# Five input buffers of their own, blank rows in four transfers, and expert 0's weights loaded during attention

## The chip, the cores and the metric

One core of one Trainium2 chip runs the whole program in one launch. The metric is device time in microseconds (us); lower is better. Three runs of the kernel before gave 385.97, 389.21 and 391.08 us; their median is 389.21 us.

## What is computed

The reference is a gated linear attention (a recurrence over time, 4 batches, 8 heads, 768 steps, head size 48) followed by a hierarchical mixture of experts over the 3072 resulting tokens of width 384. Each token goes to one of 4 groups and in it to one of 4 experts, so to one of 16 experts of inner width 1024. All data are float32.

```
for t in range(S):
    state = alpha[:, :, t, :, None] * state + einsum('bhd,bhe->bhde', k[:, :, t], v[:, :, t])
    y[:, :, t] = einsum('bhd,bhde->bhe', q[:, :, t], state)
x = y as (B*S, H*D)
...
g_idx = argmax(x @ w_group);  e_idx = argmax(x[mask_g] @ w_expert[g])
h = maximum(x @ w1[g, e], 0);  out = (softmax weight of group * of expert) * (h @ w2[g, e])
```

## The kernel before, in words

The work has two stages. The first, attention, walks over 24 chunks of 128 time steps (6 chunks for each of 4 batches; called c0 to c23 here). The second runs the experts one after the other on the rows that attention has sorted by expert into a DRAM table `slots_d`.

**A chunk.** One chunk's input is a single row block of 128 x 1925 float32 (962.5 KB): decays, keys, queries and values side by side. `load` (L452) brings it into an SBUF tile that `home` (L442) picks. VectorE then runs a backward scan of the decays (`back`, L460), a reciprocal (`turn`, L466) and a forward scan (`forth`, L471). GpSimd multiplies keys (`keys`, L476) and queries (`queries`, L480) in place, in the input tile itself. TensorE takes the scores (`scores`, L494), turned keys (L523), the rows and gate logits of an earlier chunk (`to_rows`, L583), the state's gain (L536), and the output of the chunk before: `outputs` (L560) and `from_before` (L569). VectorE or ScalarE and GpSimd mask the scores (L503; L508 and L511), and VectorE adds the gain to the state (`grown`, L545). An input tile is in use until its chunk's L569 (or L560, where a batch starts) is done.

**Sorting.** Every few chunks a group's gate is computed on VectorE (L649 to L688), TensorE counts tokens per expert (L761 to L769), and GpSimd scatters each chunk's rows to `slots_d` with an indirect DMA (L737). Before the first scatter the rows from 144 to 223 of each expert's block are filled with blanks by `fill` (L803, issued at L805).

**Buffers.** Input tiles come from two places. Chunks 0 to 5 and 10 to 23 use a pool `inp` of NIN = 6 buffers; chunks 6 to 9 borrow the four weight buffers of the pool `wp` (`HOMES`, L439), which the experts need only later. So the load of chunk n waits for chunk n-10 up to n = 15 and for chunk n-6 from n = 16 on.

**Order.** Each engine runs its instructions in program order. A planner (`Plan`, L30) lays that order out from estimated costs: `add` gives every operation an engine, a cost, what it comes after, and when a transfer lands; `order` then picks, engine by engine, the ready operation with the longest path behind it. TensorE (row "pe") and the DMA queue of SyncE (row "sp") are chained in the order in which the code adds them. On SP that order is the list `order` at L858 to L866: all loads, with `wr`, the two blank fills (before loads 9 and 11) and at the end expert 0's `w1` and `w2` (`load_w1` L255, `load_w2` L261). The DMA for chunk n is told to the planner at L870.

**Into the experts.** While the last chunks run, 96 rows of expert 0 are fetched early and run on TensorE between the last chunks (L275 into the `zs` banks). Then the fullest other expert is chosen ("ahead"), its weights are loaded and, once every scatter has landed, its rows are fetched (L789); from there TensorE runs the expert products (L275 into `bank`) without a break to the end.

The few lines that set which buffer a chunk gets, and what its load waits for:

```
HOMES = {6: "w1", 7: "w2", 8: "w1", 9: "w2"}
LATER = max(HOMES) + 1
...
o = n - (LATER if n < LATER + NIN else NIN)
dma(f"load{n}", 0.45, partial(load, chunks[n]), IW * 512,
    after=[late(o, "own_out"), late(o, "gain"), late(o, "from"), late(o, "turn_k"),
           late(o, "score")], lands=0.6 if n < LATER + NIN else 2.0)
```

## Time and profile before

| | us |
|---|---|
| median of three runs | 389.21 |
| lowest, highest | 385.97, 391.08 |
| the profiled execution's own time | 387.43 |
| its span, first to last instruction | 385.7 |
| granted TensorE clock, mean over the span | 0.994 |
| TensorE busy in the span | 370.1 (96%) |
| VectorE, ScalarE, GpSimd busy | 158.2, 118.0, 201.6 |

The profile is of one execution. Times in it run from the first instruction. "PE" is TensorE, "DVE" VectorE, "ACT" ScalarE, "POOL" GpSimd, "SP" SyncE, whose work here is to issue DMAs. A wait in square brackets is the idle time of the engine just ahead of the row, with what ended it; "issue" means that the profile shows nothing that the engine waited for.

### The profile page before, as it was taken

Reading aid. Unit: us, or ns where it says so; the run is one execution under the profiler, and the core shown is the slowest. Engines: PE = TensorE matmul, PEld = TensorE weight load, DVE = VectorE, ACT = ScalarE, POOL = GpSimd, SP = SyncE. Lnnn points to the kernel's source line nnn. Section 1 sums busy time; section 2 is a strip of 40 time slices with the busy share of each in tenths; the row PEclk is TensorE's granted clock in tenths of the full one; section 3 lists DMA queues with packets and bytes.
Section 4 is the critical chain, followed back from the end, with each engine's and each line's share of the span. In section 5 each row is a group of like instructions: output and inputs, shape, how many; then the busy total and the mean of one; then the engine's idle time right before and its main releaser. Section 6 shows DMA issues by size and latency. Waiting matters only on the chain.

```text
span 385.7 us, 9827 instructions
## 1 busy us (share of the span) xinstructions
PE 370.1 (96%) x3946; PEld 352.5 (91%) x3946; DVE 158.2 (41%) x340; ACT 118.0 (31%) x310; POOL 201.6 (52%) x239
## 2 busy tenths in 40 slices
PE   8899899999899899999999999999999999999993
PEld 5787788887689899999999999999999999999993
DVE  6799589899977402020741202022021020120120
ACT  2566476766563121111112112121111121121120
POOL 5988769989697021534426153362541632623543
PEclk9999899999999999999999999999999999999999
DMA  8999905879968697856758686586876866865400
GB/s 292 392 401 399 389 29 193 289 269 294 370 237 317 182 339 262 263 204 215 222 195 257 228 274 208 192 250 248 279 212 205 301 243 211 278 263 202 181 18 32
DMA packets 30495, 94.82 MB, mean 246 GB/s; under 512 B 17925, under 2 KB 19843, under 8 KB 26096
## 3 DMA queue, kind: packets, MB, share of 16 engines
q1 hardware_dynamic: 24560, 83.53, 62.2%
q0 software_dynamic: 4832, 9.55, 7.3%
q10 hardware_dynamic: 1056, 1.10, 0.9%
q8 instruction: 32, 0.52, 0.6%
q14 instruction: 15, 0.12, 0.1%
HBM read 82.61 MB, written 11.98 MB: 245 GB/s over the span
## 4 chain that ended last, share of the span: by engine, by line
PE 84%; POOL 5%; issue 4%; DVE 3%; DMA 1%; ACT 1%; SPq 0%; POOLq 0%; DVEq 0%
PE bank L275 63%; PE bank L583 4%; PE zs L494 4%; PE zo L560 4%; PE zs L275 2%; PE zo L569 2%; POOL in L480 2%; PE zo L523 2%; PE bank L536 1%; DMA in<-in_rows_dram 1%; DVE kd L460 1%; POOL slots_d L737 1%; POOL out_dram L1174 1%; POOL in L476 1%; DVE cq L471 1%
## 5 line engine op out<-in xcount | busy, mean ns | idle before, releaser
L1174 POOL DMA_INDIRECT out_dram<-yq,dst_q x101 | 98.1, 971 | 156.0 <-DVE yq L1170 107.3
L275 PE MATMUL bank<-hT,w 128*128 128x216 f32 (+14 forms) x720 | 120.8, 328 | 0.0
L275 PEld LDWEIGHTS bank<-hT,w 128*128 128x128 f32 x720 | 118.7, 190 | 0.0
L275 PE MATMUL bank<-xt_e,w 128*128 128x213 f32 (+14 forms) x720 | 117.4, 323 | 0.0
L275 PEld LDWEIGHTS bank<-xt_e,w 128*128 128x128 f32 x720 | 115.4, 190 | 0.0
L1200 DVE SCALAR_TENSOR_TENSOR dst_q<-xq,past_q 128x7 int32<-128x7 int32 (+1 forms) x14 | 2.3, 167 | 156.5 <-DMA out_dram<-yq,dst_q 156.5
L290 ACT ACTIVATE hT<-bank 128x432 f32<-128x432 f32 (+15 forms) x64 | 31.2, 488 | 96.1 <-PE bank L275 96.1
L306 ACT COPY yT<-bank 128x432 f32<-128x432 f32 (+29 forms) x30 | 12.1, 402 | 104.4 <-PE bank L275 104.4
L737 POOL DMA_INDIRECT slots_d<-xr,place x24 | 24.1, 1005 | 8.2 <-issue 4.8
L476 POOL TENSOR_TENSOR in<-in,kd 112x512 f32<-112x512 f32 (+1 forms) x21 | 23.8, 1136 | 5.1 <-DMA in<-in_rows_dram 2.7
L583 PE MATMUL bank<-wr,yt 112*64 112x116 f32 x384 | 25.4, 275 | 0.7 <-issue 0.4
L460 DVE TENSOR_TENSOR_SCAN kd<-in,starts 112x516 f32<-112x516 f32 (+1 forms) x21 | 24.3, 1162 | 4.0 <-DMA in<-in_rows_dram 4.0
L1167 DVE STREAM_TRANSPOSE yq<-yT 128x672 f32<-128x672 f32 (+2 forms) x16 | 12.9, 809 | 31.8 <-ACT yT L306 31.8
L494 PE MATMUL zs<-in 48*64 48x128 f32 x640 | 22.2, 272 | 3.8 <-POOL in L480 3.8
L480 POOL TENSOR_TENSOR in<-in,cq 112x512 f32<-112x512 f32 (+1 forms) x22 | 23.9, 1091 | 3.4 <-DVE cq L471 3.3
L471 DVE TENSOR_TENSOR_SCAN cq<-in,starts 112x516 f32<-112x516 f32 (+1 forms) x22 | 24.7, 1129 | 1.6
L583 PEld LDWEIGHTS bank<-wr,yt 112*64 112x64 f32 x384 | 19.7, 140 | 4.4 <-issue 0.9
L494 PEld LDWEIGHTS zs<-in 48*64 48x64 f32 x640 | 18.2, 133 | 6.0 <-POOL in L480 5.5
L560 PE MATMUL zo<-sm,in 128*48 128x128 f32 (+1 forms) x320 | 22.6, 274 | 0.4 <-ACT kt L528 0.2
L575 ACT COPY yt<-zo 112x512 f32<-112x512 f32 x24 | 14.1, 586 | 21.5 <-PE zo L569 19.9
L560 PEld LDWEIGHTS zo<-sm,in 128*48 128x48 f32 (+1 forms) x320 | 18.5, 130 | 0.5 <-issue 0.3
L511 POOL TENSOR_SCALAR_AFFINE_SELECT sm<-sm 128x512 f32<-128x512 f32 x27 | 16.9, 639 | 3.0 <-ACT sm L508 2.9
(158 smaller groups left out, 345.5 us busy)
## 6 DMA issues: line engine op xcount, KB each, us to landing
w<-in_w_dram SPq DMA_DIRECT2D x34, 1536.0 KB, 6.9
in<-in_rows_dram SPq DMA_DIRECT2D x17, 962.5 KB, 11.9
w<-in_rows_dram SPq DMA_DIRECT2D x4, 962.5 KB
xq<-slots_d SPq DMA_DIRECT2D x28, 85.8 KB, 6.2
xq<-slots_d SPq DMA_DIRECT2D x28, 73.5 KB, 6.4
slots_d<-blank SPq DMA_DIRECT2D x2, 980.0 KB
out_dram<-yq,dst_q POOLq DMA_INDIRECT x101, 4.8
in<-in_rows_dram SPq DMA_DIRECT2D x1, 704.0 KB
```

The costliest lines, as they stand in the source:

```text
L275: nc.tensor.matmul(z, lhsT=w, rhs=x, start=first, stop=last, skip_group_check=True)
L290: nc.scalar.activation(out=hT[:, f0:f0 + 2, 0:n], in_=z[:, 0:2 * n].rearrange("p (f t) -> p f t", f=2), func=AF.Relu)
L460: nc.vector.tensor_tensor_scan(out=flat(c.kd[:, p0:p1])[:, ::-1], data0=c.t[0:R, A1 * p1:A1 * p0:-1], data1=one_col.to_broadcast([R, A1 * ...
L471: nc.vector.tensor_tensor_scan(out=flat(c.cq[:, p0:p1]), data0=c.t[0:R, A1 * p0:A1 * p1], data1=starts[0:R, A1 * p0:A1 * p1], initial=1.0, ...
L476: nc.gpsimd.tensor_tensor(out=c.k[:, p0:p1], in0=c.k[:, p0:p1], in1=c.kd[:, p0:p1, 1:A1], op=ALU.mult)
L480: nc.gpsimd.tensor_tensor(out=c.q[:, p0:p1], in0=c.q[:, p0:p1], in1=c.cq[:, p0:p1, 1:A1], op=ALU.mult)
L494: nc.tensor.matmul(c.zs[i][s, p, :], lhsT=c.k[r, p, s], rhs=c.q[r, p, :], start=True, stop=True)
L511: nc.gpsimd.affine_select(out=c.sm[:, i], in_=c.sm[:, i], pattern=[[0, HP], [1, P]], compare_op=ALU.is_ge, fill=0.0, base=0, channel_multi ...
L560: nc.tensor.matmul(of(c.zo, p)[o], lhsT=c.v[:, h * D:h * D + o.stop - o.start], rhs=c.sm[:, i, p, :], start=(p < 2), stop=(c.bc == 0), ski ...
L583: nc.tensor.matmul(z[s, p * W:(p + 1) * W], lhsT=c.yt[:, p, s], rhs=wr[:, p, :], start=True, stop=True)
L737: sent = nc.gpsimd.indirect_dma_start(out=slots_by[t], out_offset=bass.IndirectOffsetOnAxis(ap=m["place"][:, c:c + 1], axis=0), in_=xr[:, ...
L1174: nc.gpsimd.indirect_dma_start(out=out_by.popleft().rearrange("n (j w) -> (n j) w", j=4), out_offset=bass.IndirectOffsetOnAxis(ap=dst[:, b ...
```

## The change

Three things change. The four borrowed buffers go (`HOMES` and `LATER`) and the pool `inp` shrinks from 6 buffers to 5, so that the load of every chunk n from 5 on waits for chunk n-5. The blank rows go out in four transfers of half the size, ahead of loads 7, 8, 9 and 10. Expert 0's `w1` and `w2`, which no longer have to wait for the borrowed buffers, are issued ahead of loads 14 and 17. The planner is told that each load lands 2.0 us after its transfer.

```
-    NIN = 6
+    NIN = 5
...
-        HOMES = {6: "w1", 7: "w2", 8: "w1", 9: "w2"}
-        LATER = max(HOMES) + 1
-
         def home(c):
             if not hasattr(c, "t"):
-                if c.n in HOMES:
-                    t = wp.tile([P, DC, F], F32, name=HOMES[c.n]).rearrange("p c f -> p (c f)")
-                else:
-                    t = inp.tile([P, IW], F32, name="in")
-                c.t, c.v = t, t[:, AW + 2 * KW:IW]
+                c.t = t = inp.tile([P, IW], F32, name="in")
+                c.v = t[:, AW + 2 * KW:IW]
...
-        FILLS = 2
+        FILLS = 4
...
-        for i, k in enumerate((9, 11)):
+        for i, k in enumerate((7, 8, 9, 10)):
             before_load(k, ("fill", i))
-        order += [("w1", 0), ("w2", 0)]
+        before_load(14, ("w1", 0))
+        before_load(17, ("w2", 0))
         for kind, n in order:
             if kind == "load":
-                o = n - (LATER if n < LATER + NIN else NIN)
+                o = n - NIN
                 dma(f"load{n}", 0.45, partial(load, chunks[n]), IW * 512,
                     after=[late(o, "own_out"), late(o, "gain"), late(o, "from"), late(o, "turn_k"),
-                           late(o, "score")], lands=0.6 if n < LATER + NIN else 2.0)
+                           late(o, "score")], lands=2.0)
```

On TensorE not one instruction changes its place; only the names of the buffers that chunks 6 to 9 are read from differ. On SP the order does change. The two pieces below are SP's queue from the load of c4 to that of c10, before and after. L454 and L448 are the same line of `load`, L805 and L799 that of `fill`; a wait on PE is the wait for an earlier chunk to leave its buffer, one on DMAHW is for an earlier transfer.

Before:

```order
L454 DMA in_295<-in_rows_dram 128x1925 [waits DMAHW5_49]
L454 DMA in_342<-in_rows_dram 128x1925 [waits DMAHW6_49]
L454 DMA w1_400<-in_rows_dram 128x1925 [waits DMAHW7_49]
L454 DMA w2_438<-in_rows_dram 128x1925 [waits DMAHW0_49]
L454 DMA w1_492<-in_rows_dram 128x1925 [waits DMAHW1_49]
L805 DMA slots_d_66<-blank_86 80x8x392 [waits DMAHW2_49,Pool_49]
L454 DMA w2_591<-in_rows_dram 128x1925 [waits DMAHW3_49]
L454 DMA in_655<-in_rows_dram 128x1925 [waits DMAHW4_49,PE_49,Pool_49]
```

After:

```order
L448 DMA in_295<-in_rows_dram 128x1925 [waits DMAHW5_49]
L448 DMA in_342<-in_rows_dram 128x1925 [waits DMAHW0_49,DMAHW6_49,PE_49,Pool_49]
L448 DMA in_402<-in_rows_dram 128x1925 [waits DMAHW2_49,DMAHW7_49,PE_49,Pool_49]
L799 DMA slots_d_66<-blank_86 80x4x392
L448 DMA in_485<-in_rows_dram 128x1925 [waits DMAHW1_49,PE_49,Pool_49]
L799 DMA slots_d_66<-blank_86 80x4x392
L448 DMA in_569<-in_rows_dram 128x1925 [waits DMAHW3_49,PE_49,Pool_49]
L799 DMA slots_d_66<-blank_86 80x4x392 [waits DMAHW4_49]
L448 DMA in_655<-in_rows_dram 128x1925 [waits DMAHW5_49,PE_49,Pool_49]
L799 DMA slots_d_66<-blank_86 80x4x392 [waits DMAHW6_49]
L448 DMA in_729<-in_rows_dram 128x1925 [waits DMAHW7_49,PE_49,Pool_49]
```

Before, the first load that waits for TensorE is that of c10; after, it is that of c5, and every fill stands behind a load that waits.

Expert 0's weights, on SP after the change, from the load of c13 to that of c17 (L255 is `w1`, L261 `w2`); before, both stand behind the load of c23.

```order
L448 DMA in_972<-in_rows_dram 128x1925 [waits DMAHW2_49,DMAHW3_49,PE_49,Pool_49]
L255 DMA w1_1032<-in_w1_dram 128x3072
L448 DMA in_1106<-in_rows_dram 128x1925 [waits DMAHW4_49,DMAHW5_49,PE_49,Pool_49]
L448 DMA in_1154<-in_rows_dram 128x1925 [waits DMAHW7_49,PE_49,Pool_49]
L448 DMA in_1249<-in_rows_dram 128x1925 [waits DMAHW0_49,DMAHW6_49,PE_49,Pool_49]
L261 DMA w2_1286<-in_w2_dram 128x3072
L448 DMA in_1358<-in_rows_dram 128x1925 [waits DMAHW1_49,PE_49,Pool_49]
```

Neither weight transfer waits for anything, so each goes out right behind the load ahead of it and stands in front of the next load's data.

On DVE the planner puts the scans of a chunk later against the other work. The pieces are DVE's queue around c12's first scan (it reads `in_782` before and `in_890` after); `sm` is the masked score of c10, `sums` the state of c9.

Before:

```order
L460 SCALAR_TENSOR_TENSOR kd_1015<-in_782,starts_118 112x516
L503 TENSOR_TENSOR sm_1039<-zs0_988,causal_68 128x512
L466 RECIPROCAL starts_118<-kd_1015 112x4
L471 SCALAR_TENSOR_TENSOR cq_1016<-in_782,starts_118 112x516
L545 TENSOR_TENSOR sums_1075<-state1_120,bank_1043 112x192
```

After:

```order
L497 TENSOR_TENSOR sm_1045<-zs0_982,causal_68 128x512
L454 SCALAR_TENSOR_TENSOR kd_1058<-in_890,starts_118 112x516
L460 RECIPROCAL starts_118<-kd_1058 112x4
L465 SCALAR_TENSOR_TENSOR cq_1059<-in_890,starts_118 112x516
L539 TENSOR_TENSOR sums_1108<-state1_120,bank_1035 112x192
```

The scan of c12 now stands behind the mask of c10 instead of ahead of it; if its load is late, the state of c9 waits behind it.

On POOL the clearing of two result buffers (L418) moves from between two of the last scatters to a place ahead of c11's keys.

## Rows read from the trace of the kernel before

**Rows 1.** Chain that ended last, in order of time: start us, us, what

```profile
132.31 242.24 PE bank L275 x1488
...
380.51 0.97 POOL out_dram L1328
```

**Rows 2.** Busy time by stage; after POOL: PEclk, DMA share, GB/s

```profile
core 0: us, PE busy (x) PEld busy (x) DVE busy (x) ACT busy (x) POOL busy (x), PEclk, DMA share, GB/s
...
30.00:40.00 10.00, 9.80 (x223) 8.57 (x221) 9.54 (x13) 6.66 (x18) 8.42 (x19) 1.00 1.03 402
...
50.00:60.00 10.00, 10.00 (x240) 8.89 (x238) 8.88 (x21) 7.12 (x24) 6.78 (x7) 1.00 0.12 43
...
90.00:100.00 10.00, 8.83 (x200) 7.58 (x189) 9.69 (x16) 6.58 (x17) 9.34 (x10) 1.00 0.94 326
```

**Rows 3.** Timeline of PE, 36 to 48 us: start us, us, instruction [idle before]

```profile
36.63 1.07 PE L494 MATMUL zs<-w 48*64 48x128 f32 x32
...
40.44 0.89 PE L494 MATMUL zs<-w 48*64 48x128 f32 x24
42.69 0.45 PE L494 MATMUL zs<-w 48*64 48x128 f32 x8 [1.36 <-issue]
...
47.95 0.29 PE L494 MATMUL zs<-w 48*64 48x128 f32 x4
```

**Rows 4.** Busy time by stage in finer cuts, columns as in rows 2

```profile
40.00:42.00 2.00, 1.33 (x33) 1.00 (x30) 0.80 (x2) 1.33 (x6) 1.93 (x9) 1.00 1.02 409
...
44.00:46.00 2.00, 2.00 (x33) 2.00 (x30) 0.00 (x0) 1.75 (x4) 1.14 (x2) 0.50 0.99 412
...
93.00:97.00 4.00, 3.28 (x69) 2.73 (x67) 3.79 (x9) 2.62 (x9) 3.78 (x5) 1.00 1.02 354
```

**Rows 5.** DMA queues, from the page

```profile
q8 instruction: 32, 0.52, 0.6%
```

**Rows 6.** Timeline of DVE, 96 to 100 us

```profile
96.24 2.95 DVE L728 TENSOR_TENSOR early_held<-seen 128x1 f32<-128x1 f32 x1
...
99.28 0.14 DVE L731 TENSOR_TENSOR seen<-seen,starts 128x1 f32<-128x1 f32 x1
```

**Rows 7.** Timeline of POOL and PE, 100 to 111 us

```profile
100.64 1.18 POOL L476 TENSOR_TENSOR in<-in,kd 112x512 f32<-112x512 f32 x1 [0.89 <-DVE kd L460]
...
103.77 1.01 POOL L737 DMA_INDIRECT slots_d<-xr,place  x1 [1.95 <-DVE xr L688]
...
110.84 1.21 PE L494 MATMUL zs<-in 48*64 48x128 f32 x32 [0.27 <-POOL in L480]
```

**Rows 8.** Timeline of POOL, 113 to 116 us

```profile
114.48 1.28 POOL L418 MEMSET yT<- 128x672 f32 x2
```

**Rows 9.** Timeline of PE, 60 to 74 us: c8's buffer free, c13 to c15

```profile
51.76 0.66 PE L569 MATMUL zo<-w,state 48*48 48x128 f32 x16
...
64.88 1.06 PE L494 MATMUL zs<-in 48*64 48x128 f32 x32
...
68.68 1.11 PE L494 MATMUL zs<-in 48*64 48x128 f32 x32
...
73.01 1.07 PE L494 MATMUL zs<-in 48*64 48x128 f32 x32
```

**Rows 10.** DMA issue of one load alone (issued at 73.3 us), us to landing

```profile
in<-in_rows_dram SPq DMA_DIRECT2D x1, 962.5 KB, 7.7
```

**Rows 11.** DMA issues, from the page: KB each, median us to landing

```profile
w<-in_w_dram SPq DMA_DIRECT2D x34, 1536.0 KB, 6.9
in<-in_rows_dram SPq DMA_DIRECT2D x17, 962.5 KB, 11.9
```

**Rows 12.** Chain, c2 from its first scan to its scores

```profile
10.33 1.15 DVE kd L460
...
14.32 1.21 PE zs L494 x31
```

## The prediction

> **What bounds the kernel now.** I read the chain that ended last first. From 132.31 us on it is one unbroken piece of expert products on TensorE, 242.24 us long, and then the last scatter to DRAM at 380.51 [rows 1]. Nothing in the change touches an instruction behind 132.31, so only the time up to there can move: about 132 of the 385.7 us of the span. Around the span lie 387.43 - 385.7 = 1.7 us.
>
> The busy time by stage comes next [rows 2]. In 30 to 40 us the DMA share is 1.03, so the DMA engines have no room at all: ten chunks' inputs and the blank rows are queued ahead of need. From 50 to 60 us they stand nearly still (0.12): every buffer is full. TensorE is busy all of 50 to 60 us, and less than all of 90 to 100 us (8.83 of 10), where the share is 0.94. So attention is bound by TensorE, whose pitch I take as the distance of the scores of c14 and c15: 73.01 - 68.68 = 4.33 us [rows 9]. What the change can give is where TensorE falls short of that pitch.
>
> There are two such places. The first is in the timeline of TensorE [rows 3]: after 24 of the 32 products of c8's scores it stands still for 1.36 us. No semaphore stands between the 24th and the 25th, and the profile names no releaser. Then it works on at half clock: the granted clock is 0.50 in 44 to 46 us, which is 1.2 instead of 2.4 GHz, after a pause in 40 to 42 us in which it was busy 1.33 of 2 us [rows 4]. From c8's scores to c9's it is 47.95 - 40.44 = 7.51 us, 3.2 over the pitch: 1.36 us of pause and 1.8 of slow clock. The DMA share there is 1.02 [rows 4].
>
> The second is on VectorE: an addition on a 128 x 1 tile takes 2.95 us, while the next one of the same shape takes 0.14 [rows 6]. Behind it stand the scans of c22 and, on GpSimd, its keys (0.89 us of waiting) and a scatter (1.95) [rows 7]. The DMA share then is again 1.02 [rows 4], as the last inputs and expert 0's weights come in together.
>
> **The change part by part.**
>
> *Five buffers, first effect: no deep queue of transfers at 40 us.* After the change SP issues at most one load for each chunk that TensorE finishes, so in 4.33 us one load (0.986 MB, 2.5 us at 402 GB/s) and in four of the intervals a fill (0.5 MB, 1.2 us): 3.7 of 4.33 us, where now it is all of it. Instructions come over the same DMA engines: the page lists a queue for them, 32 packets and 0.52 MB [rows 5]. A pause in the middle of a group that waits for nothing, with the engines full, is what a late piece of program would look like. I take the pause and the slow clock as gone: -3.2 us, with 0 and -3.2 as bounds. No other work hides them: TensorE is busy without a gap right behind them (10.00 of 10 in 50 to 60 us) [rows 2], and so it is TensorE again that is late next.
>
> The Trainium skill speaks against this: "Runtime: NRT & Kernel Launch", section "Instruction fetch mechanics", says that each sequencer fetches the next block of its program over its own DMA queue while it runs the present one, and that the cost of a block's end is mostly hidden. By that the pause is no fetch, nothing here would take it away, and the sum below would be 3.2 us higher. The trace leaves it open: it shows one pause of this kind on TensorE, and that in the stretch with the fullest queue.
>
> *Five buffers, second effect: a load has less time.* The load of c13 waits for c8's last read, which ends at 51.76 + 0.66 = 52.42, and c13's scores start at 64.88 [rows 9]: 12.5 us. What has to fit: the transfer, which for one load issued alone took 7.7 us from issue to landing [rows 10]; and two scans, a reciprocal and the query product, for c2 14.32 - 10.33 = 4.0 us from first scan to scores [rows 12]. That is 11.7, so 0.8 us are left. Shorter landings are possible: a weight transfer of 1536 KB lands in 6.9 us [rows 11], and 573.5 KB less at 402 GB/s make that 5.4 us, an estimate; then 3.1 us are left. What can go wrong stands in the order: VectorE's scan of c12 now comes behind the mask of c10, and if the load is late, the state of c9 queues behind it, for which ScalarE and TensorE's output of c10 wait. GpSimd may also have another product of 1.18 us [rows 7] ahead of the query: then 0.4 us are missing for each of the 11 chunks from c12 to c22, +4.2 us. The median landing of 11.9 us [rows 11] comes from the deep queue of today, which goes. A gain isn't possible here, for no load starts earlier. I take 0, because the row of the same transfer still fits, and keep 0 and +4.2.
>
> The Trainium skill would leave more room: "DMA: Bandwidth & Descriptors", section "Anatomy of one DMA", gives a fixed 2.0 us and the bytes at 436 GB/s, so 4.3 us for a load (an estimate from that page). By that the wait would fit with over 4 us to spare, the next term would be 0, and the sum -4.1 instead of -2.8. The row (7.7 us) says otherwise here, and the row decides.
>
> *Expert 0's weights amid attention.* Both are gone from the end of the queue, and each 1.57 MB (3.9 us at 402 GB/s) now stands in front of an input: behind the loads of c13 and c16. 2.5 + 3.9 us of transfers stand ahead of a load that is issued 4.33 us after the first of them, so the loads of c14 and c17 come about 2.1 us late. For c14 the scatters have hardly begun (share 0.12) [rows 2], so I set its landing at 5.4 + 2.1 = 7.5, which with 4.0 fits into 12.5. For c17, with scatters alongside, 7.7 + 2.1 + 4.0 = 13.8 is 1.3 us too much. I take +1.3. The bounds are 0 and both at 1.3 with the slow clock behind each pause (1.8 us) [rows 3]: +6.3.
>
> What goes at the end of the queue is worth something if VectorE's 2.95 us are also a matter of full DMA engines: 2.8 us over the 0.14 of its like, and GpSimd waited 0.89 + 1.95 = 2.8 us for it. But the loads of c22 and c23 remain in that stretch. So the bounds are 0 and -2.8, and I take a third, -0.9.
>
> *Fills and clears.* Four fills move the same bytes as two, in 1.2 us pieces that fit behind a load, and none is needed before the first scatter, which comes behind c11's keys: 0. The two clears (1.28 us) [rows 8] leave GpSimd's last scatters, but the very last scatter waits for c23's own rows, which come after them anyway: 0, at best -1.3. ScalarE's order changes by a few places and it is the least busy engine (118.0 us): 0.
>
> **Sum.** -3.2 + 0 + 1.3 - 0.9 + 0 = -2.8 us. Against the profiled execution that is 387.43 - 2.8 = 384.6. That execution lies 1.8 us below the median of the runs, 389.21, so for the median I forecast 389.2 - 2.8 = 386.4 us. Rivals are given against the median, too.
>
> **Rivals.**
>
> *The pause stays, or comes again elsewhere.* For it: only one pause is in the first 48 us, though the engines were full for most of them, so a full queue alone doesn't make one. Weights and inputs that now come together at c13 and c16 fill the engines as well. Against it: none shows in the 242 us of expert products, where the engines are less loaded. Then 3.2 us are lost from the sum: 389.2 - 0.9 + 1.3 = 389.6 us. The Trainium skill's section on instruction fetch, named above, is on this rival's side. This is the case in which the change doesn't do what it says.
>
> *All of it works.* Landings near 5.4 us, no pause at c17, and VectorE's 2.95 us go wholly: -3.2 - 2.8 = -6.0, so 383.2 us; with the clears -7.3 and 381.9. For it: both stalls lie where the DMA share is over 1. Against it: the row of 7.7 us. The Trainium skill's section on the anatomy of a DMA is on this side.
>
> *Late loads pace attention; this one is slower.* Place: VectorE's first scan of a chunk, from c12 on. Price: 0.4 us for each of 11 chunks, 4.2, and at c14 and c17 a pause of 1.3 with 1.8 of slow clock behind it, 6.3; with the pause at c8 gone, 4.2 + 6.3 - 3.2 = +7.3, so 396.5 us. If that pause stays too, 399.7. It decides from the point where landing takes more than 12.5 - 4.0 = 8.5 us, or 7.3 with a product of GpSimd ahead. For it: the row of 7.7 lies between these two. Against it: half the loads, up to c11, come before the scatters, and VectorE's order has the scans later, so that less of its other work queues behind a late load.
>
> **How the numbers follow.** My chances: the forecast (384.5 to 388.5 us) 0.50, the pause stays 0.20, all of it works 0.15, late loads 0.15. For the range I leave out the upper part of the last and the best end of the third: 381.9 to 393.5 us. Over 2% (about what a measurement of this kernel can tell from no change) is 7.8 us. Faster by that needs 381.4 or less, which is even beyond the -7.3 of all gains together: 0.05 for what I don't see. Slower by that means over 397.0: 0.07, somewhat under half of the late loads. Within 2%: 0.88.
>
> **What would show it.** Right: TensorE's 32 products of c8's scores in one piece, clock 1.00 in every slice from 40 to 50 us, c9's scores about 3 us earlier; a DMA share well under 1 between 20 and 48 us; the expert products starting near 129.5 instead of 132.31. VectorE's waits for input DMAs from c12 on would be a few tenths, and over 1 us only at c14 or c17. Wrong: if the pause is there with a share under 0.9, it isn't the queue; if VectorE waits 1 us or more for most inputs, the third rival holds; if the clock falls once more between 50 and 110 us, the weights cost more than I took.

## The result, and the profile after

The changed kernel is slower, by 0.7%, which is inside the 2% for which I had given 0.88. In 20 runs of each its median is 390.66 us (388.94 to 394.64) against 388.24 (385.52 to 391.08) for the kernel before; the ratio is 1.0071, with a 95% interval of 1.0042 to 1.0099. Ratios in this document leave out the executions that took over 1.5% more than the fastest of their kernel. I had forecast 386.4 us, 2.8 less than the median I started from. The number lies inside the range I gave (381.9 to 393.5), but the kernel moved the other way.

The profiled execution took 390.86 us, 3.43 more than the one before (0.7% of the median are 2.8 us, so about 0.7 us of the layout below is the draw of the two executions). Its chain that ended last, in order of time (start us, us, what):

```profile
23.85 8.70 DMA in<-in_rows_dram
32.64 1.24 DVE kd L454
...
37.41 7.44 DMA in<-in_rows_dram
44.95 1.23 DVE kd L454
...
49.87 0.30 DVE starts L643
...
51.65 0.26 DVE picked L658
...
52.51 1.13 DVE kd L454
...
135.75 242.24 PE bank L275 x1488
```

The expert products take 242.24 us as in [rows 1] and start 3.44 us later (135.75 for 132.31). So all of it was lost in attention, the part in which the prediction had said that the time can move. The rows above it tell of two links that were not on the path before: transfers of inputs (c7's, 8.70 us, and c10's, 7.44; between 15 and 60 us before, no input's transfer was), and from 44.95 to 57.27 us a stretch of VectorE, with the first group's gate (L643 to `picked`) between the scan of c10 and that of c11 (52.51).

The pause that the change was to remove is nearly gone. TensorE after, 41 to 59 us: start us, us, instruction, idle before (to be laid beside [rows 3]; L488 is L494 of before).

```profile
41.34 1.09 PE L488 MATMUL zs<-in 48*64 48x128 f32 x26 [0.27 <-POOL in L474]
42.80 0.44 PE L488 MATMUL zs<-in 48*64 48x128 f32 x6 [0.38 <-issue]
...
46.47 1.07 PE L488 MATMUL zs<-in 48*64 48x128 f32 x32
...
52.05 0.20 PE L755 MATMUL bank<-picked,before 128*128 128x96 bf16 x1 [1.11 <-DVE picked L658]
...
52.66 1.11 PE L488 MATMUL zs<-in 48*64 48x128 f32 x32
...
58.49 1.21 PE L488 MATMUL zs<-in 48*64 48x128 f32 x32 [0.64 <-POOL in L474]
```

c8's scores are still cut, after 26 of 32 products, but for 0.38 us instead of 1.36, and from c8's scores to c9's it is 5.13 us (46.47 - 41.34) instead of 7.51. That is 2.38 us won. Then it goes wrong: TensorE waits 1.11 us for VectorE's `picked`, 0.64 for GpSimd, and c11's scores start at 58.49 (57.30 before).

The windows show the same:

```profile
core 0: us, PE busy (x) PEld busy (x) DVE busy (x) ACT busy (x) POOL busy (x), PEclk, DMA share, GB/s
...
20.00:30.00 10.00, 9.44 (x222) 8.18 (x213) 9.04 (x13) 6.63 (x21) 9.19 (x17) 1.00 0.89 262
30.00:40.00 10.00, 9.42 (x212) 8.18 (x213) 5.85 (x8) 6.25 (x17) 5.18 (x11) 1.00 1.00 344
40.00:50.00 10.00, 9.36 (x206) 8.07 (x201) 7.35 (x12) 6.53 (x20) 9.31 (x18) 1.00 0.76 269
50.00:60.00 10.00, 7.54 (x164) 5.89 (x158) 9.48 (x24) 4.44 (x13) 6.55 (x8) 1.00 0.82 310
```

The clock is 1.00 in all four. But the DMA engines are as full in 30 to 40 us as before (1.00) while they move 344 GB/s instead of 402 [rows 2], and in 50 to 60 us TensorE is busy 7.54 of 10 us, where it had been 10.00 [rows 2].

What came in place of the pause is on VectorE, whose first scan of c7 to c10 waits for its input, 2.32 + 1.47 + 1.36 + 0.95 = 6.1 us:

```profile
32.64 1.23 DVE L454 TENSOR_TENSOR_SCAN kd<-in,starts 112x516 f32<-112x516 f32 x1 [2.32 <-DMA in<-in_rows_dram]
...
37.06 1.23 DVE L454 TENSOR_TENSOR_SCAN kd<-in,starts 112x516 f32<-112x516 f32 x1 [1.47 <-DMA in<-in_rows_dram]
...
41.21 1.23 DVE L454 TENSOR_TENSOR_SCAN kd<-in,starts 112x516 f32<-112x516 f32 x1 [1.36 <-DMA in<-in_rows_dram]
...
44.95 1.23 DVE L454 TENSOR_TENSOR_SCAN kd<-in,starts 112x516 f32<-112x516 f32 x1 [0.95 <-DMA in<-in_rows_dram]
```

These loads are slow beside the fills. The list of DMA issues (KB each, median us from issue to landing), asked for the stretch in which c7's load goes out (23 to 26 us), and for that of c12's (46 to 48 us):

```profile
in<-in_rows_dram SPq DMA_DIRECT2D x1, 962.5 KB, 8.7
slots_d<-blank SPq DMA_DIRECT2D x1, 490.0 KB, 9.7
...
in<-in_rows_dram SPq DMA_DIRECT2D x1, 962.5 KB, 4.6
```

With a fill ahead of it and one behind, a load lands after 8.7 us; with none, after 4.6. The same load shows it too: c10's takes 7.44 us here, with a fill ahead of it, and 5.0 in e2 below, where the fills go out 4 us behind it.

Laid out by the starts of the scores (after minus before), the 3.44 us are: +0.90 up to c8, -2.38 from c8 to c9, +3.49 from c9 to c12, 0 to c16, +1.30 from c16 to c17, +1.17 to c19, -0.91 to c23, -0.13 to the expert products.

The +1.30 lie where the prediction had +1.3, behind the weights, but they are not a wait for c17's input. Its load does come late: it is issued at 70.85 us, and VectorE's scan waits 1.12 us for it. TensorE, though, has no idle time ahead of c17's scores. It stops inside those of c16:

```profile
79.30 0.63 PE L488 MATMUL zs<-in 48*64 48x128 f32 x12
80.79 0.88 PE L488 MATMUL zs<-in 48*64 48x128 f32 x20 [0.86 <-issue]
81.60 0.60 PE L517 MATMUL zo<-ident,in 112*128 112x112 f32 x4
```

From the first of these scores to the products behind them (L517) it is 2.30 us; before it was 1.00 (77.29 to 78.29). That is the whole 1.30, and the chain that ended last runs through this stop and not through c17's load.

### The profile page after: what moved, and what is told of

It is laid out like the page before. It is cut to its first block, busy times and chain, and to the rows that moved or that the text cites. A ratio compares the mean times of both kernels' runs of the same rounds, so it can differ in the third digit from the quotient of the medians.

```text
span 388.9 us, 9820 instructions
## 1 busy us (share of the span) xinstructions
PE 369.7 (95%) x3946; PEld 351.5 (90%) x3946; DVE 159.2 (41%) x340; ACT 118.0 (30%) x310; POOL 201.8 (52%) x239
## 4 chain that ended last, share of the span: by engine, by line
PE 78%; DVE 9%; DMA 6%; issue 3%; POOL 2%; ACT 1%; SPq 0%; POOLq 0%; DVEq 0%; ACTq 0%
PE bank L275 62%; DMA in<-in_rows_dram 6%; PE zs L488 3%; PE bank L577 3%; PE zo L554 3%; DVE kd L454 2%; PE zs L275 2%; PE zo L563 2%; DVE cq L465 1%; PE bank L530 1%; PE zo L517 1%; DVE sm L497 1%; POOL in L474 1%; POOL out_dram L1169 1%; DVE early_held L722 1%
## 5 line engine op out<-in xcount | busy, mean ns | idle before, releaser
L306 ACT COPY yT<-bank 128x432 f32<-128x432 f32 (+29 forms) x30 | 12.1, 403 | 104.3 <-PE bank L275 104.3
L470 POOL TENSOR_TENSOR in<-in,kd 112x512 f32<-112x512 f32 (+1 forms) x25 | 28.6, 1144 | 14.2 <-DVE kd L454 8.1
L454 DVE TENSOR_TENSOR_SCAN kd<-in,starts 112x516 f32<-112x516 f32 (+1 forms) x25 | 29.4, 1180 | 11.9 <-DMA in<-in_rows_dram 11.3
L488 PE MATMUL zs<-in 48*64 48x128 f32 x768 | 28.0, 272 | 6.5 <-POOL in L474 5.3
L488 PEld LDWEIGHTS zs<-in 48*64 48x64 f32 x768 | 22.5, 133 | 9.9 <-POOL in L474 7.4
L465 DVE TENSOR_TENSOR_SCAN cq<-in,starts 112x516 f32<-112x516 f32 (+1 forms) x26 | 29.6, 1144 | 1.9
L474 POOL TENSOR_TENSOR in<-in,cq 112x512 f32<-112x512 f32 (+1 forms) x26 | 28.7, 1108 | 2.4 <-DVE cq L465 2.2
L554 PE MATMUL zo<-sm,in 128*48 128x128 f32 (+1 forms) x384 | 26.8, 274 | 0.1
L554 PEld LDWEIGHTS zo<-sm,in 128*48 128x48 f32 (+1 forms) x384 | 22.1, 130 | 0.3 <-ACT kt L522 0.3
L569 ACT COPY yt<-zo 112x512 f32<-112x512 f32 x24 | 14.1, 586 | 18.2 <-PE zo L563 16.6
L543 ACT ACTIVATE state<-sums,kd 112x48 f32<-112x48 f32 x64 | 16.9, 328 | 6.8 <-DVE sums L539 6.4
```

The lines of the kernel that those rows point to most:

```text
L454: nc.vector.tensor_tensor_scan(out=flat(c.kd[:, p0:p1])[:, ::-1], data0=c.t[0:R, A1 * p1:A1 * p0:-1], data1=one_col.to_broadcast([R, A1 * ...
L465: nc.vector.tensor_tensor_scan(out=flat(c.cq[:, p0:p1]), data0=c.t[0:R, A1 * p0:A1 * p1], data1=starts[0:R, A1 * p0:A1 * p1], initial=1.0, ...
L470: nc.gpsimd.tensor_tensor(out=c.k[:, p0:p1], in0=c.k[:, p0:p1], in1=c.kd[:, p0:p1, 1:A1], op=ALU.mult)
L474: nc.gpsimd.tensor_tensor(out=c.q[:, p0:p1], in0=c.q[:, p0:p1], in1=c.cq[:, p0:p1, 1:A1], op=ALU.mult)
L488: nc.tensor.matmul(c.zs[i][s, p, :], lhsT=c.k[r, p, s], rhs=c.q[r, p, :], start=True, stop=True)
L543: nc.scalar.activation(out=c.st[:, p, 0:D], in_=chunks[c.n - 1].sums[:, p], func=AF.Copy, scale=c.kd[:, p, 0:1])
```

## The experiments

Theory: the fills ride with the loads of c7 to c10, so that with five buffers these loads come late; VectorE loses its lead over TensorE, and the first group's gate (46 to 56 us on VectorE) then has no slack to stand in. Rivals: the order that the planner made for five buffers costs, not the buffers; the weights amid attention cost; and, for the two terms of the prediction that rest on full DMA engines, a late piece of program is not what holds TensorE or VectorE.

The runs were made on several chips, on which the kernel before took from 388 to 398.6 us, so only ratios to the kernel before on the same chip are compared (with 95% intervals). A run with one execution has a profile only. Each stretch below is read from one profiled execution.

### Six buffers (e1, e5), five with the order for six (e9)

```
e1:  inp = ...tile_pool(name="inp", bufs=NIN + 1)     (order as planned for five)
e5:  NIN = 6                                          (order planned for six)
e9:  NIN = 6, ...tile_pool(name="inp", bufs=NIN - 1)  (order for six, five buffers)
```

> The changed kernel with six input buffers instead of five; every engine's order of instructions stays as in the changed kernel, so that only the wait of a load moves from chunk n-5 to chunk n-6. In the changed kernel the first scans of c7 to c10 wait 2.3, 1.5, 1.4 and 1.0 us for their inputs. Theory A (the blank rows, sent between the loads of c6 and c10, make these loads land late): a load that starts 4.3 us earlier hides that too, scan waits under 0.5 us each, time about 388 us. Theory B (five buffers are too few whatever the transfers): the same, 388 us or less, and also c17's wait of 1.1 us goes. Theory C (the loss is in the order that the planner gave, not in the loads): the waits shrink but the time stays at 390 to 391.

> The changed kernel with six input buffers that the planner knows of, so that VectorE's order around the first group's gate is again that of the kernel before (c11's backward scan ahead of the gate). The run with six buffers and five's order gave 388.75 us, and there c10's scores to c12's still took 10.2 us, where the kernel before takes 8.1. Theory D (part of the loss is that VectorE has no scan done ahead when the first gate comes): 8.1 to 9 us from c10's scores to c12's, time 386.5 to 388. Theory A alone (only the late loads): 388.75, with 10 us there.

> Five real buffers, but the order of the instructions that the planner makes for six (VectorE's scan of c11 ahead of the first gate, as before the change). With e1 (six buffers, order for five) and e5 (six and six) it completes a table of two by two. Theory A (the loads' lateness costs, the order only passes it on): c7 to c10 wait for their inputs as after the change (sum about 6 us), c9 to c12 takes 15.5 us or more, ratio to the kernel before 1.004 to 1.010. Theory B (the order costs, five buffers would do): c10 to c12 takes about 8.1 us, c9 to c12 about 13 us, ratio 0.998 to 1.002.

| ratio to before | five buffers | six buffers |
|---|---|---|
| order for five | after: 1.0071 (1.0042 to 1.0099) | e1: 1.0006 (0.9971 to 1.0042) |
| order for six | e9: 1.0154 (1.0099 to 1.0209) | e5: 0.9996 (0.9948 to 1.0043) |

The sixth buffer takes away 0.65 per cent with the one order and 1.6 with the other. With six buffers the two orders are alike in time, within about 0.6 per cent, and with five the order made for five is the better one (e9 has four runs; it came out above the 1.004 to 1.010 that I had expected). In e9's profile VectorE waits 0.77 us for c7's load and 3.44 for c8's:

```profile
30.32 1.23 DVE L454 TENSOR_TENSOR_SCAN kd<-in,starts 112x516 f32<-112x516 f32 x1 [0.77 <-DMA in<-in_rows_dram]
36.72 1.23 DVE L454 TENSOR_TENSOR_SCAN kd<-in,starts 112x516 f32<-112x516 f32 x1 [3.44 <-DMA in<-in_rows_dram]
```

So the rival "order" falls as the main cause: with it and six buffers the loss is gone from the time. Its true part: c10 to c12 takes 8.08 us in e5, as before, and still 10.2 in e1; from c9 on it is 13.1 before and in e5, 15.2 in e1, and 16.6 after. Up to 2.1 of the 3.49 us lost there thus come with the order even where there is a sixth buffer, a size that the intervals of e1 and e5 can't exclude. And e9, with the order for six, takes 16.9 there. What belongs to the late loads and what to the order in this stretch is not separated.

### The fills elsewhere (e2, e3)

```
e2:  -  fill i ahead of the loads of c7, c8, c9, c10
     +  all four fills behind the load of c11
e3:  +  all four fills ahead of the load of c5
```

> The changed kernel with its four fills sent behind the load of c11 instead of between those of c6 and c10; five buffers, all engine orders but SP's as in the changed kernel. Theory A: the scans of c7 to c10 no longer wait (sum under 1.5 us instead of 6.1), c11's scores come 2 us or more earlier than 58.5, and the time falls by 1.5 to 3 us, unless the fills then hold up c12 and the first scatter by as much. Theory B: the waits stay at 1 us or more for each of c7 to c10 and the time at 390 to 391. Theory C: waits gone, time unchanged.

> The changed kernel with its four fills sent ahead of the load of c5, all else as in the changed kernel. Theory A: c5 and c6 land late (c5's scan waits 2 us or more, since about 2 MB go ahead of it) and c7 to c10 in time, so the loss is the same or up to 2 us smaller: 389 to 391. Theory B: c7 to c10 still wait 1 us or more each, and c5's lateness comes on top: 391 to 394. Theory C: 390 to 391.

e2: 1.0026 (0.9986 to 1.0065), which overlaps with the kernel after. The scans of c7 to c10 wait 2.05 us in all instead of 6.1 (I had expected under 1.5). No pause of TensorE over 0.18 us is left, and c9's scores start at 44.16 (46.47 after, 47.95 before); part of the loss comes back behind the fills, where c10 to c12 takes 12.1 us. e3, with four runs: 1.0136 (1.0077 to 1.0194); theory A had 389 to 391 us, and it is 393.3. The loss moves with the fills to c5, whose scan waits 5.51 us, and there the pause, in c4's scores, is longer than any before:

```profile
23.00 0.62 PE L491 MATMUL zs<-in 48*64 48x128 f32 x10
25.71 1.55 PE L491 MATMUL zs<-in 48*64 48x128 f32 x22 [2.09 <-issue]
```

The granted clock in 25 to 30 us is 0.54, so nearly all at 1.2 GHz. The same 2 MB cost most where they meet the loads that TensorE needs next.

### Expert 0's weights back at the end (e4), and both placements undone (e13)

```
e4:  -  w1 ahead of the load of c14, w2 ahead of that of c17
     +  both behind the load of c23
e13: e2 and e4 together, five buffers
```

> The changed kernel with expert 0's weights at the end of the queue, behind the load of c23, as in the kernel before; all engine orders but SP's as in the changed kernel. Theory A and B leave the loss up to c12 as it is; c17's scan no longer waits 1.1 us and c16 to c17 takes 5.0 instead of 6.3 us, so the time falls by about 1.3 us, to 389.4, and not to 388.2. If the weights cost nothing in the middle: 390.7. If they cost more (c13 to c19 together): down to 388.

> Five buffers, all fills behind the load of c11, expert 0's weights behind the load of c23. If what e2 and e4 regained adds up: e2's 1.0026 less the 0.0018 that e4 gained over the kernel after, so about 1.001 (0.997 to 1.005), with c7 to c10 waiting under 1 us in all and c16 to c17 about 5.0 us. If the sixth buffer is what counts: still 1.004 or more, with waits of VectorE for inputs from c11 on.

e4: 1.0053 (1.0016 to 1.0089). From c16's scores to c17's it is 5.03 us as before the change, and 6.33 after it; VectorE's wait at c17 is gone, and so is the stop in c16's scores. The ratio can't be told from that of the kernel after. c17 to c19 stays long (9.34 us, 8.79 after, 7.62 before), so the +1.17 there are not the weights'; I did not trace them further. e13: 1.0000 (0.9966 to 1.0035), where adding up e2 and e4 had given 1.001. With five buffers, then, undoing both placements takes the loss away; what each is worth alone is within the noise.

e13 also shows that the weights' late load and the +1.30 are two things. I had expected about 5.0 us from c16 to c17, and it is 6.51: c17's scan does not wait for its input, but c16's scores stop at the same place as after the change, with the weights at the end of the queue. In e7 below it is the other way round: weights amid attention, c17's scan waits 0.94 us for its input, c16's scores run in one piece, and c16 to c17 takes 5.03 us. e13 first, then e7 (TensorE, and VectorE's scan of c17):

```profile
77.02 0.62 PE L493 MATMUL zs<-in 48*64 48x128 f32 x12
78.69 0.88 PE L493 MATMUL zs<-in 48*64 48x128 f32 x20 [1.05 <-issue]
...
79.32 1.07 PE L488 MATMUL zs<-in 48*64 48x128 f32 x32
80.32 0.60 PE L517 MATMUL zo<-ident,in 112*128 112x112 f32 x4
79.02 1.23 DVE L454 TENSOR_TENSOR_SCAN kd<-in,starts 112x516 f32<-112x516 f32 x1 [0.94 <-DMA in<-in_rows_dram]
```

With five buffers and the weights amid attention the stop is there in the kernel after, e3, e6, e9 and e16 (0.34 to 1.04 us; 1.94 in e10) and not in e2, e7 and e15; c16 to c17 takes 5.8 to 6.5 us in the former (10.5 in e10, with the clock at 0.50 behind the stop) and 5.0 to 5.1 in the latter.

### The gate elsewhere in VectorE's order (e6, e7)

```
e6:  the first gate after c11's scan; its counts four places later on TensorE
e7:  e6, and the fills planned ahead of the load of c12
```

> The changed kernel, five buffers and fills where they are, but the first gate on VectorE stands behind c11's backward scan, and TensorE counts the first group one chunk later (after c9's output instead of c8's), so that the gate has more time. Theory D: c10's scores to c12's 8.5 to 9.5 us instead of 10.4, c9's to c10's 4.3 instead of 6.2, time 388 to 389.5. Theory A alone: the scans of c7 to c10 wait as before and the time stays at 390 to 391.

> The same as the run before this one, with the four fills behind the load of c11 as well; five buffers. Theories A and D together: both losses go, no scan from c7 to c10 waits over 0.5 us, no pause of TensorE over 0.4 us up to 45 us, and the time is 386 to 388, unless the fills hold up c12, c13 and the first scatter, which costs up to 2 us: 388 to 389.5.

e6: 1.0127 (1.0064 to 1.0189); e7: 1.0052 (1.0009 to 1.0096). Both miss the gain that I had expected of theory D, and neither is clear of the kernel after. With the gate later, c9 to c10 takes 4.5 us in e6, near the pitch, but c11 to c12 takes 7.1 (7.45 in e7): the wait only moved by a chunk or two. These two places for the gate, then, do not give back the lead that late loads have cost.

### What stops TensorE (e14, e15)

```
-        WARM = (27, 5)
+        WARM = (23, 5)          and 14 products of 128 x 64 behind the 23
```

> The kernel before with four of the 27 warming products at the start left out and 14 small ones (128 x 64) added: TensorE's program is ten products longer ahead of everything else, and nothing else changes. If a late piece of TensorE's program makes the pauses: the one in c8's scores after 24 of 32 products comes after 14, and the one in c6's rows after 4 of 16 leaves that line for the scores or the outputs ahead of it. If they belong to the operations or their operands: after 24 and after 4 as before.

> The same shift in the kernel after. Its pauses at c8's scores (after 26 of 32), c17's (after 12) and c7's L563 (after 4 of 16) come ten products earlier if they belong to places of the program: after about 16 of 32, after 2, and in the group ahead of L563. Otherwise at 26, 12 and 4 again.

In the kernel before, the pauses are at c8's scores after 24 products [rows 3] and in the rows behind c5's scores after 4 of 16 (the expectation calls them c6's rows):

```profile
28.93 0.42 PE L583 MATMUL bank<-wr,yt 112*64 112x116 f32 x4
29.79 0.82 PE L583 MATMUL bank<-wr,yt 112*64 112x116 f32 x12 [0.43 <-issue]
```

With ten products more at the start of its program, e14 shows (TensorE, L497 are scores):

```profile
28.25 1.06 PE L497 MATMUL zs<-in 48*64 48x128 f32 x26
30.17 0.44 PE L497 MATMUL zs<-in 48*64 48x128 f32 x6 [0.85 <-issue]
...
41.51 0.66 PE L497 MATMUL zs<-w 48*64 48x128 f32 x14
43.72 0.82 PE L497 MATMUL zs<-w 48*64 48x128 f32 x18 [1.55 <-issue]
```

24 became 14; and 4 of the rows became 26 of the 32 scores ahead of them, which is ten earlier too. The pauses sit at places of the program, not at operations. In e15 one pause is left, 0.89 us in the outputs ahead of c7's scores:

```profile
33.34 0.61 PE L557 MATMUL zo<-sm,in 128*64 128x128 f32 x7
34.84 0.76 PE L557 MATMUL zo<-sm,in 128*64 128x128 f32 x9 [0.89 <-issue]
```

That is after 7 of 16 products of this group. In the kernel after, the pause ahead of c7's scores (0.34 us) lies after the first product of the next group, not the fourth as my expectation had it, and so after 17 from the start of this one: ten again. Those in the scores of c8 and c16 (the expectation calls the latter c17's) were under 0.18 us in that execution.

What TensorE waits for at these places shows in the list of DMA queues. The kernel before, asked for 40.0 to 40.5 us, and e13, asked for 76.0 to 76.5 us, each show one 16 KB packet on the queue of instructions:

```profile
q8 instruction: 1, 0.02, 12.9%
...
q8 instruction: 1, 0.02, 12.0%
```

The two packets start at 40.1 and 76.35 us, and TensorE goes on at 42.69 and 78.69, 2.6 and 2.3 us later. Of 39 stops of 0.34 us or more, without a releaser and up to 122 us, in the 20 traces 36 end 2.2 to 2.8 us after the start of such a packet; the other three stand ahead of a whole group of scores. So a piece of program that comes late is what TensorE waits for. Why it comes late is not settled: e13's stop of 1.05 us follows on two microseconds with a DMA share of 0.36, and e3's of 1.13 us at c17 on 0.54.

### What holds VectorE (e10, e16, e17)

```
e10: eight more clears of a small tile at the start of VectorE's program
e16: -  tensor_tensor(out=early_held, in0=seen[:, t1, 0:1], in1=seen[:, 0, 0:1], subtract)
     +  tensor_scalar(out=early_held, in0=seen[:, t1, 0:1], scalar1=0.0, add)   (seen[:, 0, 0] is 0)
e17: the same edit in the kernel before
```

> VectorE gets eight more clears of a small tile at the very start, where it waits for the first input; nothing else changes. Theory A (a block of VectorE's program comes late): the hold of about 2.3 us leaves the addition into early_held (then 0.15 to 0.3 us) and stands about eight instructions of VectorE earlier, at the reduction lg or the scan ahead of it. Theory B (that addition itself, or what it reads, is slow): the hold stays on early_held with 1.9 to 2.4 us. TensorE's pauses stay at the same instructions under both, because its program is the same. The time is that of the kernel after within its scatter (1.003 to 1.010 of before).

> The kernel after with the addition into early_held reading one tile from SBUF and a constant in place of two tiles; the same place in VectorE's order. If VectorE waits for an access to SBUF that GpSimd's chain of products holds: early_held takes 0.1 to 0.3 us, and the next operation with two operands in SBUF (picked, 0.24 us) takes the wait over, about 2 us, until GpSimd's first mask ends. If early_held's own result or place were slow: still 1.8 to 3.0 us there. The time: as the kernel after (1.004 to 1.010 of before) under both.

> The kernel before with the addition into early_held reading one tile in SBUF and a constant. The hold of 2.95 us goes (early_held 0.15, nothing takes it over). If the bound -2.8 of the prediction is the truth: ratio 0.993. If, as e16's scores suggest (c21 to c23 8.6 us where the kernel after has 9.6), about 1 us of it reaches TensorE: 0.997 (0.995 to 0.999). If other work hides it: 1.000.

In e10 the hold stayed on `early_held` (1.84 us), eight instructions further into the program than it had been. The clears were not free, as I had thought (0.39 us each, and c0's scores started 3.3 us late), so its time, 404.21 us, says nothing here. What does hold it stands beside it on GpSimd. After the change, VectorE first, then GpSimd (cut at 103.7 us, so that only the first mask is in the row):

```profile
101.50 2.37 DVE L722 TENSOR_TENSOR early_held<-seen 128x1 f32<-128x1 f32 x1
103.79 0.24 DVE L658 TENSOR_TENSOR picked<-oh,starts 128x96 bf16<-128x96 f32 x1
```

```profile
100.94 1.19 POOL L470 TENSOR_TENSOR in<-in,kd 112x512 f32<-112x512 f32 x1
102.08 1.18 POOL L474 TENSOR_TENSOR in<-in,cq 112x512 f32<-112x512 f32 x1
103.21 0.63 POOL L505 TENSOR_SCALAR_AFFINE_SELECT sm<-sm 128x512 f32<-128x512 f32 x1
```

The hold ends at 103.87, GpSimd's mask at 103.84. In the kernel before it is 99.19 and 99.17. In all 15 traces with a hold of 1.84 us or more it ends within 0.03 us of the end of that mask; in e3 and e7 the addition came later against GpSimd's work and took 0.19 and 0.31 us. Full DMA engines have no part in it: in e1 the hold lasts 1.92 us with a DMA share of 0.05 (17 GB/s):

```profile
99.93 1.92 DVE L722 TENSOR_TENSOR early_held<-seen 128x1 f32<-128x1 f32 x1
99.93:101.85 1.92, 1.77 (x42) 1.35 (x37) 1.92 (x3) 1.22 (x5) 1.92 (x4) 1.00 0.05 17
```

With one operand in SBUF instead of two, e16 has:

```profile
102.75 0.15 DVE L722 TENSOR_SCALAR early_held<-seen 128x1 f32<-128x1 f32 x1
102.86 0.25 DVE L658 TENSOR_TENSOR picked<-oh,starts 128x96 bf16<-128x96 f32 x1
```

The hold is gone, though one of GpSimd's products runs beside it (from 102.04 us, 1.19 us long). `picked`, which also has two operands in SBUF, did not take it over, as I had expected; why the one is held and the other not stays open. In the kernel before, the same edit (e17) gave 0.9963 (0.9926 to 1.0001), about 1.4 us and just not clear of no change; c20 to c23 went from 16.30 to 14.94 us.

### What beats both (e8, e11, e12, e18)

```
e8, e11: NIN = 6, the four fills behind the load of c11
e12:     e8, and expert 0's weights behind the load of c23
e18:     e12, and e16's early_held
```

> Six buffers that the planner knows of and the four fills behind the load of c11, weights behind the loads of c13 and c16 as in the changed kernel. Theories A and D together: the best of these, 385.5 to 387.5; if the fills hold up the loads behind them, 388. If buffers and fills are not what matters: 390 to 391.

> The kernel of e8 once more (six buffers, all four fills behind the load of c11), with more rounds. If it beats the kernel before as e8 said: ratio 0.991 to 0.999. If e8 was the luck of its runs: 0.999 to 1.003.

> e8 with expert 0's weights behind the load of c23 in place of amid attention. If the 1.3 us at c17 that the weights cost with five buffers are also there with six: c16 to c17 about 4.3 to 5.0 us, ratio 0.3 per cent under that of e11. If the sixth buffer hides the late load already: the same ratio as e11 within 0.2 per cent, and c16 to c17 alike in both.

> Six buffers, fills behind the load of c11, expert 0's weights behind the load of c23, early_held with one operand in SBUF. If the parts add up: e12's 0.9947 less about 1 us, so 0.992 (0.988 to 0.996). If the tail behind attention takes the gain back (a scatter or a fetch that comes when it comes): as e12, 0.993 to 0.998.

e8: 0.9955 (0.9912 to 0.9999); e11, the same kernel on another chip with more runs: 0.9988 (0.9963 to 1.0012), so a gain of this kernel is not sure. e12: 0.9947 (0.9915 to 0.9979), beside e11 on one chip, with overlapping intervals. c16 to c17 takes 5.03 us in both, so what lies between them is not from there; and though e12's scores of c23 start 3.2 us earlier (108.59 for 111.75), the expert products of the two profiled executions end within 0.4 us of each other. A gain in attention need not reach the end. e18: 0.9904 (0.9863 to 0.9944), about 3.8 us under the kernel before, the lowest ratio of all. It still has a pause:

```profile
48.58 0.61 PE L532 MATMUL bank<-in,kt 128*64 128x48 f32 x16 [2.99 <-issue]
```

The four fills go out from 35.58 us on, the DMA share is 0.95 or more from 38 to 50 us, and the granted clock is 0.50 in 50 to 56 us behind the pause. In e12, with fills at nearly the same time, no pause over 0.18 us is seen. Whether a better place for the blank rows would give these 3 us back was not tried.

## Why the prediction was wrong, step by step

**Only the part before the expert products can move: right.** 242.24 us on both sides.

**Five buffers, first effect, -3.2: right in kind.** It gave -2.38 from c8 to c9, clock 1.00 throughout. The cause that I only argued, a piece of program that comes late, is shown now: e14 moved two pauses by ten products by moving the program by ten, and the stops end 2.2 to 2.8 us after a packet of instructions starts. I had read one such pause in the first 48 us of the trace before; there are three (0.43 and 0.20 us besides the 1.36). That full DMA engines make the program late is only in part borne out. In e2 the pauses went when the fills left, but the stops of e13 and e3 with a share of 0.36 and 0.54 ahead of them are what I had named as a sign against the queue. The rival "the pause stays, or comes again elsewhere" came true in part as well: 0.86 us in c16's scores. The Trainium skill ("Runtime: NRT & Kernel Launch", "Instruction fetch mechanics"), which I had set against this, says that the cost of a block's end is mostly hidden. In these runs it is not: up to 2.99 us (e18).

**Five buffers, second effect, 0 (bounds 0 and +4.2): this is the step that failed,** together with the fills' "0, pieces that fit behind a load". I compared 12.5 us with 7.7 us of landing (of a load that went out among scatters) and 4.0 of work at c13, where no fill is near, and let the fills fit by their bytes (2.5 + 1.2 of 4.33 us). But a load with a fill on either side lands after 8.7 us; 8.7 + 4.0 = 12.7 is more than 12.5. That is the point I had named for the third rival (8.5 us). It was passed at c7 and c8 (8.7 and 8.9 us), not at c12 and c13 (4.6), and from there on once more at c17, about 9 us, where TensorE did not wait for it. The lateness also did not cost a few tenths per chunk: it used up VectorE's lead, and the first gate, which until then had stood in this lead, came to lie on the path, as the chain after shows. Measured: +0.90 up to c8 and +3.49 from c9 to c12, 4.4 us in place of 0. Up to 2.1 of them come with the new order even with a sixth buffer (e1). In time the sixth buffer takes the loss away (1.0006), and so do later fills with the weights at the end (e13, 1.0000); later fills alone (e2, 1.0026) are not clear of either. The figures of the Trainium skill's "Anatomy of one DMA" ("DMA: Bandwidth & Descriptors") are a fit for transfers that GpSimd issues, while SyncE issues these loads; they make 4.3 us for such a load, an estimate. The 4.6 us measured with no fill alongside is near it, the 8.7 us shows how far it is off when transfers share the engines.

**Weights amid attention, +1.3: right in number, by luck.** It was +1.30 from c16 to c17 and nothing at c14, and c17's load did come late, by about what I had worked out. But that lateness did not reach TensorE: the 1.30 are a stop of 0.86 us, and what follows it, inside c16's scores. In e7 the same lateness cost nothing, and e13 has the stop with the weights at the end. Whether the weights make the stop likelier is not shown.

**VectorE's hold, -0.9: wrong.** It is 2.37 us after instead of 2.95. I took a full DMA share as its cause because it stood beside it; in e1 it is there with a share of 0.05. It ends with GpSimd's mask and goes when the addition reads one operand (e16, e17). Why it lasts over several GpSimd operations stays open. Its worth, about 1.4 us (e17), lay inside my bounds. That c19 to c23 got 0.91 us shorter, the size I had forecast, is luck: the hold is only 0.58 shorter.

**Clears and ScalarE, 0:** not tried alone.

With the measured sizes the sum is -2.38 + (0.90 + 3.49) + 1.30 + 1.17 - 0.91 - 0.13 = +3.44 us instead of -2.8. Of the rivals, "late loads pace attention" named the mechanism and its threshold; I gave it 0.15, because I weighed it at the wrong chunks. What the 1.17 us from c17 to c19 are stays open.

## What to carry to other kernels

When a ring of buffers gets shorter, work out the time from a buffer's release to the use of its next content for the chunks at which other transfers go out, with the landing that such company gives, and not for a quiet stretch. A lead of one engine over another is a reserve: see which piece of work stands in it before spending it. A loss of the forecast size at the forecast place can still have another cause: see which engine waited, and for what. Of a stall beside a full resource, ask for a run that moves the one without the other before pricing it.

## What the runs showed of the hardware

- TensorE can stop for 0.3 to 3.0 us with no semaphore to wait for. The stops are at fixed places of its program (they move with it, e14) and end 2.2 to 2.8 us after a 16 KB packet of instructions starts (36 of 39 stops). Their length differs from run to run: c8's was 1.36 us before, 0.38 after, none in e2. A DMA share near 1 stands ahead of most of them, but not of all (0.36 in e13). After 2.09 us in e3 the clock fell to 1.2 GHz; in the 3 us behind a stop of 1.97 us in e11 it stayed at 1.00.
- A VectorE operation on 128 x 1 elements with two operands in SBUF can be held up to 2.95 us beside a chain of GpSimd operations, until one of them ends; with one operand it takes 0.15. The Trainium skill ("SBUF — State Buffer", "SBUF: two separate sides") tells of a pair of SBUF ports that both engines share, and that one side keeps for a whole instruction. The ends agree (within 0.03 us in 15 traces); that the hold outlasts the products of 1.18 and 1.19 us and ends only with the mask goes beyond what it says.
- Full DMA engines don't mean much data: a share of 1.03 moved 402 GB/s with a deep queue of loads [rows 2], 1.00 moved 344 with loads and fills mixed.
